# A four-layer linear-attention and memory-attention kernel: keys projected one tile ahead, weight remainders and memory updates moved, key features turned inside the next projection

## The chip, the cores and the metric

The kernel runs on one core of one Trainium2 chip. The metric is the device time of one execution in microseconds (us), the median of several runs; lower is better. TensorE (PE) multiplies matrices into eight PSUM banks; VectorE (DVE), ScalarE (ACT) and GpSimd (POOL) read, scale and write the results; SyncE (SP) issues most of the DMAs, the rest are issued by ACT and POOL. Each engine works through its own instructions in the order in which they are written, and waits on semaphores of the others.

## The reference

Four residual layers, A, B, A, B, act on x of 2048 tokens by 640 channels, with 32 heads of 20 channels:

```python
def _A_ref(x, wqkv, wo):                      # linear attention, no mask
    q, k, v = ...                             # x @ wqkv, by head
    phi = lambda t: jnp.where(t > 0, t + 1, jnp.exp(t)) + 1e-6
    pq, pk = phi(q), phi(k)
    kv = jnp.einsum("bhsd,bhse->bhde", pk, v)
    z = jnp.einsum("bhsd->bhd", pk)
    num = jnp.einsum("bhqd,bhde->bhqe", pq, kv)
    den = jnp.einsum("bhqd,bhd->bhq", pq, z)[..., None] + 1e-6
    return (num / den).reshape(B, S, D) @ wo
def _B_ref(x, wq, wk, wv, wo, beta):          # four segments of 512 tokens
    M, z = 0, 0                               # memory, 20 x 20 for a head
    for s in range(4):
        a_dot = softmax(qs @ ks.T * scale + causal_mask) @ vs
        a_mem = (phi(qs) @ M) / (phi(qs) @ z + 1e-6)
        outs.append(g * a_mem + (1 - g) * a_dot)
        M = M + phi(ks).T @ vs;  z = z + sum(phi(ks))
    return concat(outs) @ wo
x = x + _A_ref(_layernorm(x), A_wqkv, A_wo);  x = x + _B_ref(_layernorm(x), B_wq, ..., B_beta)
x = x + _A_ref(_layernorm(x), A_wqkv, A_wo);  x = x + _B_ref(_layernorm(x), B_wq, ..., B_beta)
```

## The kernel before

**Arithmetic.** The large products run on pairs of 16-bit parts. An operand is split into an upper half (ACT rounds it to 16 bits) and a lower half (DVE subtracts the upper from the original), and three of the four partial products are summed in PSUM: 15 matmuls for a tile of 128 tokens by 320 columns (line 416), or for 128 columns by 512 tokens (line 401). So a result goes PE, ACT, DVE, and only then can PE use it. Transposes, the weighing of values and the update of the memory are 32-bit matmuls.

**Stages.** The opening (0 to about 250 us) loads and splits the eight weight matrices and meanwhile does the first half of layer A: for each segment of four tiles, `g_first` projects keys (`keys(i)`) and queries (`queries(i)`), turns them into features, writes the queries' features to DRAM (`pqd`), and sums the product of features and inputs (`memory()`, line 592). After the last segment `merge` makes from that sum a 640 by 640 matrix `wm`. `a_second` reads the features back (`pqi`), normalizes and transposes them, multiplies by `wm` (line 416 with `wm,oT`) and adds the residual (`xo`, line 495). Layer B runs in the same stretch, segment by segment: `b_project` makes values, queries and keys, stores queries and keys to DRAM (`split_store`), and `attention` takes eight groups of four heads for a segment in slots of three stretches (table `STRETCHES`): row maxima (PE line 1026, DVE line 1032), scores (PE line 1067, ACT line 1071, POOL line 1078), weighing (`weigh`, line 1094), evacuation and normalizing (lines 1100 to 1118). Then comes layer A a second time (keys and queries about 760 to 1090 us, the first part of it beside the attention's last groups), and layer B again.

**The memory.** In `b_project` for each of five column tiles t, a query tile is projected, then the key features `pkT` of the tile before are transposed (`pk_turn`, line 884, copied by ACT at line 886), the key tile t is projected, and the memory of tile t-1 is updated (`update`, 16 small 32-bit matmuls, line 894, added to `acc` by DVE, lines 898 and 900). The fifth tile's turn and update are done by `rest()`, which the next segment's `a_second` draws in; there `masked` also copies `acc` into one of two buffers `mems` (line 751), which `read_mem` multiplies by the queries of the next segment.

**Order.** PE's order is exactly the order in which the program's two generators, `dense` (projections) and `attend` (attention slots), are drawn: each step returns a cost, and the generator with the lower total goes next. The other engines are ordered by a scheduler, from that order and estimated times; `high_priority` moves an instruction in it, and `issue_after` ties it behind another one on its engine.

**The handover.** At the end of the opening, the split of the last weight matrix, B's `wo`, has its five DVE lower halves (line 274, `w_Bo`) put late by `high_priority(offset=-1500)`; then it is written to DRAM as `wd_Bo` (line 279), and `open_b` waits for the last of them: one DVE memset of `one`, and six DMAs that write constant rows into the three key stacks `ks` (lines 847 to 850). These lines and `a_second`'s loads of `xo` (line 344) all stand in SP's queue.

Of the kernel before, what the change touches and what calls it, by code (L numbers as in the profile page):

```python
# [21 lines left out]
P = 128  # L22
# [122 lines left out]
class Kernel:  # L145
# [18 lines left out]
    def setup(self):  # L164
# [12 lines left out]
        self.mems, self.mn = [cp.tile([P, MW], F32, name=f"mem{j}") for j in range(2)], 0  # L177
# [56 lines left out]
    def w_prep(self, key, stage, w, wait=0, behind=None):  # L234
# [35 lines left out]
        for cols in (slice(0, HN), slice(HN, D)) if key == ("A", "k") else (slice(0, D),):  # L270
            for c in range(C):
                nc.scalar.activation(w[:, c, 0, cols], st[:, c, cols], AF.Copy, scale=scl)
                with self.tc.high_priority(offset=-1500) if key == ("B", "o") else nullcontext():
                    self.last = self.parted = nc.vector.scalar_tensor_tensor(w[:, c, 1, cols], st[:, c, cols], scl, w[:, c, 0, cols],
                                                               op0=OP.mult, op1=OP.subtract)
# [3 lines left out]
        nc.sync.dma_start(wd, w)  # L279
        self.wd[key] = wd  # L280
        yield 0.0
# [264 lines left out]
    def g_first(self, s, box, w, L, behind=None):  # L546
# [70 lines left out]
        if L["G"] is None and L["early"]:  # L617
# [123 lines left out]
    def masked(self, acc):  # L741


        mem = self.mems[self.mn % 2]
        self.mn += 1
# [97 lines left out]
    def open_stacks(self):  # L843
        nc = self.nc
        self.ks = [self.bp.tile([P, 2, SEG], F16, name=f"ks{j}") for j in range(3)]
        one = self.bp.tile([P, 2, SEG], F16, tag="nat", name="one", bufs=2)
        nc.vector.memset(one[:2], M_ONE)
        for k in self.ks:
            for a in (60, 124):
                nc.sync.dma_start(k[a:a + 2], one[:2])  # L850
# [15 lines left out]
    def b_project(self, st):  # L866
# [14 lines left out]
        def pk_turn():  # L881
# [3 lines left out]
            pk = bp.tile([P, SEG], F32, tag="pkt", name="pkt", bufs=1)  # L885
# [15 lines left out]

        for t in range(C):
# [17 lines left out]
            if pk is not None:  # L920
                update(t - 1, pk)
                yield 4 * 4 * E3 * COL
        st["projected"] = True

        def rest():
            if s == 0:
                yield from pause(4)
            if s < NSEG - 1:
                pk = pk_turn()
                yield 440  # L930
                update(C - 1, pk)
                yield 4 * 4 * E3 * COL
                st["mem"] = self.masked(acc)
        st["rest"] = rest()

# [187 lines left out]
    def attention(self, segs):  # L1123
# [3 lines left out]
        while n < NSEG * NG or prev or old:  # L1127
# [8 lines left out]
            for stretch in STRETCHES:  # L1136
                for op, k, back in stretch:
# [19 lines left out]
                    elif op == "sum":  # L1157
                        self.weigh(G, k)
# [266 lines left out]
```

## Time and profile before

| | |
|---|---|
| median of 3 runs (lowest, highest) | 1675.09 us (1674.74, 1676.49) |
| the profiled execution's own time, its span | 1673.65 us, 1671.6 us |
| PE busy | 1620.9 us (97%), 13818 matmuls |
| DVE, ACT, POOL busy | 1264.7 us (76%), 993.8 us (59%), 503.6 us (30%) |
| chain that ended last | PE 71%, DVE 14%, ACT 8%, DMA 3% |

The span runs from the first to the last instruction. A busy share is a mean over stages with different limits; PE's idle time is the rest of its row, 50.7 us. In rows of waits stand the engine and line that waited, the one it waited for, the total in us, how often, and the longest. In rows of the timeline stand the start in us, the length in us, the engine, the line, the operation, what it writes and reads, the shape, how many, and in brackets the engine's idle time before it and what ended it. In rows of windows stand the stretch, its length and for each engine the busy time, and then the clock that the throttle granted to PE (1.00 is full speed), the DMA engines' busy share and GB/s.

### The profile page before, as it was taken

The page shows a single profiled execution, that of the slowest core. Times are in us where ns is not written, and L with a number is a line of the kernel's source. Part 1 is how long each engine was busy: PE and PEld are TensorE (multiplying, and loading weights), DVE is VectorE, ACT ScalarE, POOL GpSimd, SP SyncE. Part 2 cuts the span into 40 slices and gives each one's busy share as a digit, 9 for nine tenths or more (in the row PEclk, how much of TensorE's full clock was granted, in tenths as well). Part 3 has the DMA queues.
Part 4 walks back from the last instruction along what each step waited for, and adds up shares of the span by engine and source line. Part 5 has one row for each costly group of instructions (what it writes and reads, how often), then busy time and mean ns, then how long its engine had stood idle before and what let it go on. Part 6 is the DMA issues. An engine that isn't in the chain of part 4 may idle for free.

```text
span 1671.6 us, 37870 instructions
## 1 busy us (share of the span) xinstructions
PE 1620.9 (97%) x13818; PEld 1016.7 (61%) x13818; DVE 1264.7 (76%) x4015; ACT 993.8 (59%) x1888; POOL 503.6 (30%) x1046
## 2 busy tenths in 40 slices
PE   8999998999999999999999999999999999999999
PEld 6767766464465566556557777765546646645555
DVE  7787896497887788769874465947889889878773
ACT  6666542357657647667666554333775676676673
POOL 4442241012323323433341210310232233232452
PEclk9999999999999999999999999999999999999999
DMA  6415654422322331461211303433232333323422
GB/s 223 158 53 188 220 199 173 141 98 75 118 73 71 125 115 61 137 205 56 81 45 45 114 33 125 180 98 128 78 113 90 108 95 109 108 85 105 147 100 96
DMA packets 110514, 190.98 MB, mean 114 GB/s; under 512 B 14188, under 2 KB 69868, under 8 KB 107768
## 3 DMA queue, kind: packets, MB, share of 16 engines
q1 hardware_dynamic: 97704, 142.68, 26.3%
q0 software_dynamic: 3264, 24.91, 4.2%
q10 hardware_dynamic: 9360, 20.98, 3.3%
q8 instruction: 109, 1.79, 0.4%
q14 instruction: 77, 0.63, 0.1%
HBM read 109.32 MB, written 78.64 MB: 112 GB/s over the span
## 4 chain that ended last, share of the span: by engine, by line
PE 71%; DVE 14%; ACT 8%; DMA 3%; issue 2%; POOL 1%; SPq 1%; ACTq 0%; DVEq 0%; POOLq 0%
PE ps L416 29%; PE ps L401 13%; PE ps L1094 8%; PE ps L592 4%; PE ps L1067 4%; PE ps L333 3%; ACT pe L1071 3%; PE ps L1026 3%; DVE ps L1032 3%; PE ps L469 2%; PE ps L1107 1%; DVE e L433 1%; DVE wmx L246 1%; DMA x<-in_A_x 1%; DVE pk L555 1%
## 5 line engine op out<-in xcount | busy, mean ns | idle before, releaser
L1032 DVE CUSTOM_DVE_ANT_0 ps<-ps,maskw 128x384 f32<-128x384 f32 (+3 forms) x1024 | 472.6, 520 | 31.7 <-PE ps L1026 27.4
L1071 ACT ACTIVATE pe<-ps,lsc 128x512 f32<-128x512 f32 x640 | 394.3, 694 | 82.1 <-PE ps L1067 66.7
L1078 POOL TENSOR_SCALAR_AFFINE_SELECT pe<-pe 128x256 f32<-128x256 f32 (+1 forms) x640 | 229.5, 364 | 412.5 <-ACT pe L1071 409.3
L416 PEld LDWEIGHTS <-xT 128*128 128x128 f16 x2880 | 279.8, 98 | 109.8 <-issue 4.5
L416 PEld LDWEIGHTS <-oT 128*128 128x128 f16 x1920 | 185.2, 98 | 87.3 <-issue 7.8
L1094 PE MATMUL ps<-pe,v 128*32 128x512 f32 (+3 forms) x2048 | 156.0, 436 | 7.7 <-ACT pe L1071 2.4
L416 PE MATMUL ps<-wm,oT 128*128 128x320 f16 x960 | 142.6, 301 | 4.5 <-DVE oT L338 4.2
L416 PE MATMUL ps<-w_Bo,oT 128*128 128x320 f16 x960 | 141.5, 299 | 3.8 <-ACT oT L337 2.0
L592 PE MATMUL ps<-pk,xs 128*128 128x321 f16 (+1 forms) x960 | 139.0, 302 | 5.2 <-DVE pk L555 2.5
L1032 DVE DVE_READ_ACCUMULATOR2_ANT mg<- 128x1 f32 x1024 | 143.9, 140 | 0.1
L401 PE MATMUL ps<-xT,w_Bq 128*128 128x512 f16 x600 | 140.9, 380 | 1.3 <-ACT pe L1071 0.8
L416 PE MATMUL ps<-w_Ak,xT 128*128 128x320 f16 x960 | 138.3, 299 | 1.5 <-DVE xT L338 0.9
L401 PE MATMUL ps<-xT,w_Bk 128*128 128x512 f16 x600 | 138.5, 379 | 1.2 <-ACT pe L1071 1.2
L416 PE MATMUL ps<-w_Bv,xT 128*128 128x320 f16 x960 | 139.3, 299 | 0.1
L416 PE MATMUL ps<-w_Aq,xT 128*128 128x320 f16 x960 | 137.8, 299 | 0.0
L1067 PE MATMUL ps<-qs,ks 62*128 62x512 f16 (+3 forms) x1024 | 129.5, 299 | 3.6 <-ACT pe L1071 2.2
L592 PEld LDWEIGHTS <-xs 128*128 128x128 f16 x960 | 93.4, 98 | 45.2 <-issue 3.0
L1026 PE MATMUL ps<-ks,qs 60*128 60x512 f16 (+3 forms) x1024 | 115.8, 297 | 3.0 <-DVE oT L338 1.8
L433 DVE SCALAR_TENSOR_TENSOR e<-e,r 128x320 f32<-128x320 f32 x128 | 68.1, 533 | 58.7 <-ACT r L432 58.2
L857 DVE SCALAR_TENSOR_TENSOR nat<-ps,nat 128x512 f16<-128x512 f32 x80 | 55.1, 689 | 65.3 <-ACT nat L856 65.0
L1094 PEld LDWEIGHTS ps<-pe,v 128*32 128x32 f32 x2048 | 62.9, 109 | 65.8 <-issue 47.0
L401 PEld LDWEIGHTS <-w_Bk 128*128 128x128 f16 x600 | 57.0, 98 | 67.3 <-issue 7.1
(202 smaller groups left out, 2367.0 us busy)
## 6 DMA issues: line engine op xcount, KB each, us to landing
x<-xn ACTq DMA_DIRECT2D x48, 320.0 KB
qs<-qd SPq DMA_DIRECT2D x128, 120.0 KB
ks<-kd SPq DMA_DIRECT2D x128, 120.0 KB
xo<-x SPq DMA_DIRECT2D x48, 320.0 KB
pqi<-pqd SPq DMA_DIRECT2D x32, 320.0 KB
qd<-nat SPq DMA_DIRECT2D x40, 256.0 KB
kd<-nat SPq DMA_DIRECT2D x40, 256.0 KB
x<-in_A_x SPq DMA_DIRECT2D x16, 320.0 KB
```

The source lines that it names most:

```text
L333: nc.tensor.transpose(pt[:, (c - c0) * P:(c - c0 + 1) * P], src[:, c * P:(c + 1) * P], self.ident)
L401: nc.tensor.matmul(p, w[:, c, a, t * P:(t + 1) * P], xT[:, c, b, :], start=k == 0, stop=k == 3 * C - 1)
L416: nc.tensor.matmul(p, xT[:, c, a, i * P:(i + 1) * P], w[:, c, b, n * HN:(n + 1) * HN], start=k == 0, stop=k == 3 * C - 1)
L433: nc.vector.scalar_tensor_tensor(e, e, 1.0, r, op0=OP.min, op1=OP.add)
L592: nc.tensor.matmul(p, xs[:, i, a, c * P:(c + 1) * P], pk[i][:, b, cols], start=i == 0 and a == b, stop=i == NT - 1 and a == 1)
L857: nc.vector.scalar_tensor_tensor(nat[:, 1], p, QK_SHIFT, nat[:, 0], op0=OP.mult, op1=OP.subtract)
L1026: nc.tensor.matmul(bs[par][:, a:a + n], qs[r, p, i * P:(i + 1) * P], ks[r, p, :n], start=True, stop=True)
L1032: nc.vector.tensor_tensor_reduce(bs[par][:, a:a + n], bs[par][:, a:a + n], self.maskw[:, SEG - n:], 1.0, NEG, OP.add, OP.max, G["mg"][:, p ...
L1067: nc.tensor.matmul(b[:, a:a + n], ks[r, p, j * P:(j + 1) * P], qs[r, p, j * P:], start=True, stop=True)
L1071: nc.scalar.activation(e, b, AF.Exp, scale=self.lsc)
L1078: self.select = nc.gpsimd.affine_select(d, d, pattern=pat, compare_op=OP.is_ge, fill=0.0, base=0, channel_multiplier=-1)
L1094: nc.tensor.matmul(G["pv"][32 * h4:32 * h4 + 32, j * P:], v[j][:, h * E1:h * E1 + 32], G.pop((p, par, j)), start=j == 0, stop=j == 2, skip ...
```

## The change

1. **Keys ahead** (`g_first`, all segments except the very first): the order k0 q0 k1 q1 k2 q2 k3 q3 becomes k0 k1 q0 k2 q1 k3 q2 q3. The last segment, whose queries 2 and 3 are drawn by `merge`, goes k0 k1 q0 k2 q1 k3.
2. **Handover**: the five lower halves of B's `wo` become `lower_parts()`, drawn last in the opening and tied behind the first turn of `a_second`'s tile 0. `wd_Bo` is no longer written. The three key stacks are filled whole by three POOL memsets, in place of a DVE memset and six DMAs.
3. **Updates**: a turned key tile's update is put on a list (`give`). The list is emptied in `attention` right after the last `weigh` of a group, and before a `pk_turn` where two updates are waiting (`take(1)`). `pkt` has two buffers in place of one.
4. **Turn**: `pk_turn` stands between the first 9 and the last 6 matmuls of the next key projection, not ahead of it. `rest()` has a pause between the turn and the copy `masked`.
5. `mems`, two buffers, becomes one, `mem`.

```diff
@@ w_prep @@
                 nc.scalar.activation(w[:, c, 0, cols], st[:, c, cols], AF.Copy, scale=scl)
-                with self.tc.high_priority(offset=-1500) if key == ("B", "o") else nullcontext():
-                    self.last = self.parted = nc.vector.scalar_tensor_tensor(w[:, c, 1, cols], ...
+                if key == ("B", "o"):
+                    continue
+                self.last = nc.vector.scalar_tensor_tensor(w[:, c, 1, cols], ...
...
+        if key == ("B", "o"):
+            self.remaining = (w, st, scl)
+            return
         wd = self.dr.tile([P, C, 2, D], F16, name="wd_%s%s" % key)
         nc.sync.dma_start(wd, w)
...
+    def lower_parts(self):
+        w, st, scl = self.remaining
+        behind = self.lower
+        for c in range(C):
+            with self.tc.high_priority(offset=-1500), self.tc.issue_after(behind.ins):
+                self.nc.vector.scalar_tensor_tensor(w[:, c, 1], st[:, c], scl, w[:, c, 0], op0=OP.mult, op1=OP.subtract)
+        yield 0.0
@@ g_first @@
+        yield from keys(0)
         for i in range(NT - 1):
-            yield from keys(i)
+            yield from keys(i + 1)
             if s < NSEG - 1 or i < 2:
                 yield from queries(i)
-        yield from keys(NT - 1)
@@ open_b @@
-        with self.tc.issue_after(self.parted.ins):
-            self.open_stacks()
...
-        one = self.bp.tile([P, 2, SEG], F16, tag="nat", name="one", bufs=2)
-        nc.vector.memset(one[:2], M_ONE)
         for k in self.ks:
-            for a in (60, 124):
-                nc.sync.dma_start(k[a:a + 2], one[:2])
+            self.nc.gpsimd.memset(k, M_ONE)
@@ b_project @@
-            pk = bp.tile([P, SEG], F32, tag="pkt", name="pkt", bufs=1)
+            pk = bp.tile([P, SEG], F32, tag="pkt", name="pkt", bufs=2)
...
+        def give(t, pk):
+            self.given.append(lambda: update(t, pk))
...
+            made = self.proj_t(xT, w["k"], t)
+            yield next(made)
             if pkT is not None:
+                yield self.take(1)
                 pk = pk_turn()
                 yield 440
-            p = yield from self.proj_t(xT, w["k"], t)
+            p = yield from made
...
             if pk is not None:
-                update(t - 1, pk)
-                yield 4 * 4 * E3 * COL
+                give(t - 1, pk)
...
             if s < NSEG - 1:
+                yield self.take(1)
                 pk = pk_turn()
                 yield 440
-                update(C - 1, pk)
-                yield 4 * 4 * E3 * COL
+                give(C - 1, pk)
+                yield 0.0
+                yield from pause(8)
+                yield self.take(0)
                 st["mem"] = self.masked(acc)
...
+    def take(self, keep):
+        n = len(self.given) if len(self.given) > keep else 0
+        for _ in range(n):
+            self.given.pop(0)()
+        return n * 16 * E3 * COL
@@ attention @@
                         self.weigh(G, k)
+                        if k == 2:
+                            self.take(0)
@@ opening @@
-                aux = chain(prep(("B", "k"), False), prep(("B", "o")), last(), self.a_head(L, 0, box))
+                aux = chain(prep(("B", "k"), False), prep(("B", "o")), last(), self.a_head(L, 0, box), self.lower_parts())
```

On PE the change adds and removes nothing: the same 13818 matmuls stand in another order. On the other engines it moves instructions at three places.

**Place one: VectorE at the end of the opening's second segment.** L555 and L568 are the same line of the two kernels, the lower half of a key tile's features (`pk`); L433 and L446 finish a feature, L582 and L595 add 1e-6 to a query's; L614 and L627 take the first product of `memory()`. Before:

```order
L433 SCALAR_TENSOR_TENSOR e<-e,r 128x320
L555 SCALAR_TENSOR_TENSOR pk<-e,k_scl,pk 128x320
L433 SCALAR_TENSOR_TENSOR e<-e,r 128x320
L555 SCALAR_TENSOR_TENSOR pk<-e,k_scl,pk 128x320
L433 SCALAR_TENSOR_TENSOR e<-e,r 128x320
L582 TENSOR_SCALAR e<-e 128x320
L433 SCALAR_TENSOR_TENSOR e<-e,r 128x320
L582 TENSOR_SCALAR e<-e 128x320
L614 TENSOR_TENSOR v_81<-ps,v_81 128x321
```

And now:

```order
L568 SCALAR_TENSOR_TENSOR pk<-e,k_scl,pk 128x320
L257 TENSOR_REDUCE wm_1402<-ps 1x1
L446 SCALAR_TENSOR_TENSOR e<-e,r 128x320
L595 TENSOR_SCALAR e<-e 128x320
L446 SCALAR_TENSOR_TENSOR e<-e,r 128x320
L595 TENSOR_SCALAR e<-e 128x320
L446 SCALAR_TENSOR_TENSOR e<-e,r 128x320
L595 TENSOR_SCALAR e<-e 128x320
L446 SCALAR_TENSOR_TENSOR e<-e,r 128x320
L595 TENSOR_SCALAR e<-e 128x320
L627 TENSOR_TENSOR v_80<-ps,v_80 128x321
```

Between the last key's lower half and `memory()` stand four halves of queries, where two stood.

**Place two: VectorE and SyncE at the handover.** `wm` is the merged matrix, `oT` the transposed features of `a_second`, `xn` its result. VectorE before:

```order
L274 SCALAR_TENSOR_TENSOR w_Bo<-stage,scl_Bo,w_Bo 128x640
L734 SCALAR_TENSOR_TENSOR wm<-ps,wm 128x320 x2
L338 TENSOR_TENSOR oT<-ps,oT 128x3x128
L338 TENSOR_TENSOR oT<-ps,oT 128x2x128
L847 MEMSET one 2x1024
L766 TENSOR_TENSOR pqi<-pqi,z 128x640
L770 TENSOR_REDUCE rca<-pqi 128x32
```

VectorE now:

```order
L747 SCALAR_TENSOR_TENSOR wm<-ps,wm 128x320 x10
L351 TENSOR_TENSOR oT<-ps,oT 128x3x128
L351 TENSOR_TENSOR oT<-ps,oT 128x2x128
L351 TENSOR_TENSOR oT<-ps,oT 128x3x128
L293 SCALAR_TENSOR_TENSOR w_Bo<-stage,scl_Bo,w_Bo 128x640
L778 TENSOR_TENSOR pqi<-pqi,z 128x640
L293 SCALAR_TENSOR_TENSOR w_Bo<-stage,scl_Bo,w_Bo 128x640
L782 TENSOR_REDUCE rca<-pqi 128x32
L508 SCALAR_TENSOR_TENSOR xn<-ps,ioG,xo 128x320
L783 TENSOR_SCALAR rca<-rca 128x32
L351 TENSOR_TENSOR oT<-ps,oT 128x2x128
```

The five lower halves of `w_Bo` have left the row of `wm` and stand among the first tiles of `a_second`. SyncE before:

```order
L756 DMA pqi<-pqd_0_96 128x640 x4
L279 DMA wd_Bo<-w_Bo 128x6400
L850 DMA ks_3346<-one 2x1024 x2
L850 DMA ks_3347<-one 2x1024 x2
L850 DMA ks_3348<-one 2x1024 x2
L344 DMA xo<-in_A_x 128x640 x4
```

Now `xo` follows the loads of `pqi` at once; nothing stands between them.

**Place three: ScalarE in an attention slot beside a projection.** `oTf` is the evacuation of a group, `nat` the first read of a finished projection, `e` and `r` its features. Before:

```order
L1100 ACTIVATE oTf<-ps,cg 128x512
L856 ACTIVATE nat<-ps 128x512
L1071 ACTIVATE pe<-ps,lsc 128x512
L440 ACTIVATE e<-ps,inv_Bk 128x512
L442 ACTIVATE r<-ps,inv_Bk 128x512
```

Now:

```order
L1119 ACTIVATE oTf<-ps,cg 128x512
L890 ACTIVATE pkt<-ps 128x512
L860 ACTIVATE nat<-ps 128x512
L1090 ACTIVATE pe<-ps,lsc 128x512 x2
L453 ACTIVATE e<-ps,inv_Bk 128x512
```

The copy of the turned key features, which stood behind the `nat` of the query projection before, stands ahead of the `nat` of the key projection. On PE the 30 updates stand in 21 blocks where they stood in 30: 9 blocks hold two, and 10 blocks stand directly behind the last matmuls of a weighing.

More of the change, by code (lines that the diff above doesn't have):

```diff
@@ L176, in setup @@
         self.blk = cp.tile([P, MW], BF16, name="blk")
-        self.mems, self.mn = [cp.tile([P, MW], F32, name=f"mem{j}") for j in range(2)], 0
+        self.mem = cp.tile([P, MW], F32, name="mem")
         self.wd, self.inv, self.scl, self.io = {}, {}, {}, {}
@@ L741, in masked @@
     def masked(self, acc):
[L744 to L745 removed]
+        mem = self.mem
         for (rel, t0, t1), c in zip(RUNS, (0, 0, 1, 1, 2, 2, 3, 3, 3)):
```

13 lines of the change are left out of this document (5 added, 8 removed).

## The prediction

> **What bounds the kernel now.** I read the page first, then PE's waits, then the stretches around the longest of them.
>
> ```profile
> span 1671.6 us, 37870 instructions
> PE 1620.9 (97%) x13818; PEld 1016.7 (61%) x13818; DVE 1264.7 (76%) x4015; ACT 993.8 (59%) x1888; POOL 503.6 (30%) x1046
> ...
> PE 71%; DVE 14%; ACT 8%; DMA 3%; issue 2%; POOL 1%; SPq 1%; ACTq 0%; DVEq 0%; POOLq 0%
> ```
>
> PE is busy for 97% of the span and carries 71% of the chain that ended last. Since the change gives PE the same matmuls, it can only win from PE's 50.7 us of idle time, and from matmuls that run slower than they could. The table of PE's waits says where the idle time lies:
>
> ```profile
> PE ps L416 <- DVE oT L338: 5.0, 6, 2.4
> PE ps L592 <- DVE pk L555: 2.5, 3, 2.0
> PE ps L1094 <- ACT pe L1071: 2.4, 6, 0.7
> PE ps L894 <- ACT pe L1071: 2.4, 6, 0.4
> PE ps L894 <- ACT pkt L886: 2.3, 6, 0.4
> PE ps L401 <- ACT pe L1071: 2.0, 5, 0.4
> PE ps L884 <- DVE pkT L443: 1.3, 2, 1.0
> PE ps L592 <- ACT pk L568: 0.8, 1, 0.8
> PE ps L333 <- DVE acc L898: 0.7, 2, 0.3
> PE ps L1094 <- DVE acc L900: 0.5, 2, 0.3
> ```
>
> No single wait is large; those that name this change's lines (338 at the handover, 555 and 568, 894, 884, acc) come to some 15 us. Behind two of them lies a second loss, which shows only in the granted clock:
>
> ```profile
> 111.00:114.50 3.50, 3.02 (x16) 1.93 (x17) 2.65 (x6) 2.23 (x5) 0.92 (x2) 0.74 0.00 0
> 114.50:118.00 3.50, 3.50 (x21) 2.15 (x20) 2.11 (x8) 0.10 (x1) 1.12 (x2) 0.77 0.25 94
> 252.00:253.50 1.50, 0.27 (x2) 0.15 (x3) 1.50 (x4) 0.00 (x0) 0.00 (x0) 0.71 0.82 290
> 253.50:257.00 3.50, 3.50 (x19) 2.19 (x18) 3.17 (x7) 0.21 (x1) 0.07 (x1) 0.64 1.04 267
> 870.00:1090.00 220.00, 219.51 (x1724) 158.03 (x1719) 135.96 (x309) 110.82 (x232) 45.55 (x91) 1.00 0.28 97
> ```
>
> Each row ends with PE's granted clock, DMA's share and GB/s. The clock falls after the two longest pauses. Clock lost: 3.5 x 0.26 + 3.5 x 0.23 = 1.7 us at 111, and 1.5 x 0.29 + 3.5 x 0.36 = 1.7 us at 252. The last row is layer A's second time: 0.5 us of 220 idle, so reordering can win nothing there.
>
> [...] A closed pause is therefore worth more than its length.
>
> **The change part by part.**
>
> *Keys ahead.* The long pause at 111 us is the end of the second segment, where `memory()` waits for the last key tile:
>
> ```profile
> 102.92 4.24 PE L416 MATMUL ps<-w_Aq,xT 128*128 128x320 f16 x30
> 107.00 1.40 PE L592 MATMUL ps<-pk,xs 128*128 128x321 f16 x9
> 109.21 0.31 PE L592 MATMUL ps<-pk,xs 128*128 128x321 f16 x1 [0.82 <-ACT pk L568]
> 111.48 4.86 PE L592 MATMUL ps<-pk,xs 128*128 128x321 f16 x22 [1.96 <-DVE pk L555]
> 109.19 2.23 DVE L555 SCALAR_TENSOR_TENSOR pk<-e,k_scl,pk 128x320 f16<-128x320 f32 x1 [0.63 <-ACT pk L568]
> 108.84 1.41 POOL L500 TENSOR_TENSOR xs<-xh,xs 128x640 f16<-128x640 f32 x1
> ```
>
> The last key's projection ended at 102.9, its first lower half was ready at 111.4; DVE was late, and that half itself took 2.23 us beside a POOL subtraction. Thirty query matmuls, 4.1 us, covered it. Now sixty stand there, 8.2 us: 4.1 us more cover against 0.82 + 1.96 = 2.78 us of waiting. DVE's queue between holds two query halves more, but behind the last key's half, so they don't delay it. Value: -2.8 for the pauses and -1.7 for the clock, -4.5. Bounds: -4.5, and 0 if DVE is later by as much as the cover grew. I take -4.4. In the other segments of both A layers the same wait is 0.2 us or not there; there I take 0, with +-1.5 for the part at 760 to 870 us that shares ACT and DVE with attention.
>
> *Handover.* In the order of time, PE, DVE and SP:
>
> ```profile
> 253.23 3.30 PE L416 MATMUL ps<-wm,oT 128*128 128x320 f16 x13 [2.38 <-DVE oT L338]
> 265.85 2.04 PE L416 MATMUL ps<-wm,oT 128*128 128x320 f16 x13 [1.84 <-DVE oT L338]
> 251.04 0.87 DVE L274 SCALAR_TENSOR_TENSOR w_Bo<-stage,scl_Bo,w_Bo 128x640 f16<-128x640 f32 x1
> 252.63 0.87 DVE L338 TENSOR_TENSOR oT<-ps,oT 128x384 f16<-128x384 f32 x2
> 264.31 1.01 DVE L495 SCALAR_TENSOR_TENSOR xn<-ps,ioG,xo 128x320 f32<-128x320 f32 x2 [6.69 <-DMA xo<-in_A_x]
> 251.98 0.32 SPq L279 DMA_DIRECT2D wd_Bo<-w_Bo  x1
> 254.60 4.88 SPq L850 DMA_DIRECT2D ks<-one  x6
> 259.53 5.38 SPq L344 DMA_DIRECT2D xo<-in_A_x  x4
> ```
>
> First pause: four `w_Bo` halves, 0.8 us or more each, stand between the `wm` halves ahead of `oT`. Without them `oT` is at most 3.2 us earlier, but no earlier than the last `wm` product lets it: I leave 0.3 us of the 2.38, so -2.1 and, with no long pause, -1.7 of clock. Second pause: DVE sat 6.69 us for `xo`, whose loads SP issued only at 259.53, behind `wd_Bo` and six small DMAs that waited for the memset; PE ran on until the next `oT` stood behind that. SP now goes from `pqi` straight to `xo`, with neither the store nor the six DMAs between. So -1.84. The five halves cost 5 x 0.87 = 4.4 us of DVE among the first tiles, less than its 6.69 us of idle time there. What waits now: `xn` stands ahead of the second part of tile 1's `oT` on DVE, so if `xo` were late, PE would still stall; `xo` was 4.8 us from its first issue to its use, and is needed once the first tile's two halves are multiplied, 30 matmuls of 0.14 us or 4 us in, so I keep +0.5. Sum -5.1; bounds -5.6 and 0.
>
> The three memsets of `ks` go on POOL, ahead of the second tile's 1/sigma, and start once the last `w_Bo` half has freed the memory under them. Their price is not in the trace; the nearest rows:
>
> ```profile
> L684 POOL MEMSET kt<- 128x128 f16 x10 | 2.1, 215 | 7.4 <-PE ps L592 7.2
> L1258 POOL MEMSET mem<- 128x756 f32 x2 | 1.4, 728 | 0.0
> ```
>
> By elements (0.73 to 0.95 ns each) 1024 take 0.85 to 1.0 us, by bytes (2048 of them) 0.6: 1.8 to 3.0 us for three. Nearest is the large one, by elements: 3 us. PE turns that tile only after the next one's 30 matmuls, over 4 us: 0, at worst +1.
>
> [...]
>
> *Updates and turns.* Rows of layer B: an update straight after a projection, one in an attention slot, and the same point of a slot that has no update:
>
> ```profile
> 311.02 3.40 PE L401 MATMUL ps<-xT,w_Bk 128*128 128x512 f16 x15
> 314.35 0.65 PE L894 MATMUL ps<-v,pkt 128*32 128x63 f32 x32
> 1229.69 0.65 PE L894 MATMUL ps<-v,pkt 128*32 128x63 f32 x32 [0.40 <-ACT pe L1071]
> 1216.20 2.10 PE L401 MATMUL ps<-xT,w_Bq 128*128 128x512 f16 x9 [0.40 <-ACT pe L1071]
> ```
>
> - `rest()`: turn, copy and update follow each other, six waits for the copy. The pause and the list put other matmuls between: -2.3.
> - Turns that wait for `pkT`, twice, 1.3: nine matmuls of 0.22 us, 2 us, now stand ahead of them: -1.3.
> - Updates that wait for `pe`, 2.4: the last two rows show that this pause takes whatever comes at this point, an update or, without one, the next query projection. It is a wait for a bank of PSUM. I expect it to pass to the projection: 0, at best -2.4. The same question stands for the banks that `acc` frees (0.7 + 0.5): half, -0.6.
> - Entering the small tiles: 15 matmuls at 0.216 us are 3.24, the update began after 3.33; 0.09 us each. 30 entries become 21, of which 10 follow a weighing, which uses the same 32-column tiles: between 9 and 19 x 0.09, I take -1.3.
> - Against it: turns and updates now take banks while a key projection still holds one, and the update delays the next row maxima by its 0.58 us. By the rows above a missing bank costs 0.40. 24 turns and 10 updates are so placed: 0 to 34 x 0.40 = 13.6. Where updates move to, right after a weighing, the slot's earlier banks have been read, so I take the low part, +2.
>
> Sum of this part -3.2. The single `mem` makes `masked` wait for the reads of the old memory, but the code has it behind them already: 0.
>
> **Sum.** -4.4 - 5.1 - 3.2 = -12.7 us, against the profiled execution's own 1673.65 (span 1671.6 and 2.05 around it): 1660.95. That execution was 1.44 us below the median of the runs, 1675.09, so for a median I predict 1675.09 - 12.7 = 1662.4.
>
> **The rivals.**
>
> - *Layer B nets nothing.* [...] As a mechanism of this kernel: all the 0.4 us pauses are for banks, and each passes to the next matmul that needs one. For it: the twin rows above. Against it: `pkt` and `pkT` are waits for data. Only the opening is won, -9.5: 1665.6. 17%.
> - *The handover only moves its stall.* `xo` comes late all the same, since DMA is 82% to 104% busy from 252 to 257 us, and five `w_Bo` halves hold up `oT`; the clock falls again. -12.7 + 5.1 = -7.6: 1667.5. 13%.
> - *Keys ahead don't help.* DVE stays behind by the added query work: -12.7 + 4.4 = -8.3: 1666.8. 8%.
> - *Slower: the held bank.* Each of the 34 turns and updates put inside an open key projection or ahead of the row maxima stalls PE for a bank. At 0.7 us, the longest wait of a weighing for ACT, that is 23.8 in place of my +2: -12.7 - 2 + 23.8 = +9.1: 1684.2. It decides from 0.53 us each, where 18 us cancel the 14.7 and exceed 0.2%. Against it: the pause at 0.40 is the same wherever it occurs. 10%.
>
> **How the numbers follow.** My forecast has 52%, with a range of its own of 1657 to 1668. A difference of 0.2%, 3.35 us, is about what a measurement of this kernel tells from no change: faster is below 1671.7, slower above 1678.4. Faster: nearly all of the forecast (50), most of the first three rivals (28 of 38): 0.78. Same: the remainder of these and a third of the held bank, 0.13. Slower: 0.09. The low end, 1656, is the forecast with the bank pauses and the whole of the entries won (-3) and layer A's -1.5, and a little of the bank price; the high end, 1674.5, is the handover's rival with 7 us of bank pauses. Outside lie about 2 in 10.
>
> **What would show it.** Right: no fall of the clock at 111 and 252 us, no wait of line 592 for `pk` over 0.3 us in the second segment, `xo` issued before 255 us, rows "894 <- pkt" and "884 <- pkT" gone, and "401 <- pe" grown to about 4 us in 11. Wrong: a clock below 1.00 after 20 us, a pause at the second or third tile of `a_second` for `oT` or `xn`, new waits of lines 884 and 401 for `pe` of more than 2 us in all, or row maxima (1026, 1032) late behind updates.

## The result, and the profile after

The changed kernel takes 1662.97 us (median of 5 runs, 1662.16 to 1665.72), the kernel before 1675.09 us beside it: 0.9927 of its time, 95% interval 0.9914 to 0.9940. The prediction was 1662.4 us. A second measurement (below) gave 1664.01 us; over all ten runs the median is 1663.6. The execution profiled here was the longest of its five, 1665.72 us; the last section says why.

In the changed kernel's profile the lines around the change stand 4 to 19 higher: 416 is 429, 401 is 414, 592 is 605, 333 is 346, 884 is 888, 894 is 898, 1067 is 1086, 1071 is 1090, 1094 is 1113. The head of its page and its chain:

```profile
span 1664.0 us, 37840 instructions
PE 1618.3 (97%) x13818; PEld 1020.6 (61%) x13818; DVE 1256.1 (75%) x4014; ACT 994.3 (60%) x1888; POOL 508.5 (31%) x1048
...
PE 76%; DVE 11%; ACT 7%; issue 2%; DMA 2%; POOL 1%; SPq 0%; ACTq 0%; DVEq 0%; POOLq 0%
```

PE's idle time fell from 50.7 to 45.7 us, and its busy time, with the same matmuls, by 2.6; of the chain that ended last it carries 76% where it carried 71%, VectorE 11% where it was 14%. What it waits for now:

```profile
PE ps L1113 <- ACT r L455: 6.2, 7, 1.3
...
PE ps L414 <- ACT pe L1090: 2.8, 7, 0.4
PE ps L1113 <- ACT pe L1090: 2.6, 7, 0.5
PE ps L346 <- ACT pe L1090: 2.2, 5, 0.5
...
PE ps L346 <- POOL pqi L786: 1.5, 1, 1.5
...
PE ps L429 <- DVE oT L351: 0.9, 4, 0.4
PE ps L888 <- ACT pe L1090: 0.7, 2, 0.4
...
PE ps L605 <- DVE pk L568: 0.5, 1, 0.5
```

The waits that the change aimed at are gone or small: for `oT` 5.0 before, 4.2 of it at the handover, and 0.9 now, none of it there, for `pk` 2.5 and 0.5 (at 39 us, in the first segment, whose order stayed), for `pkt` (2.3) and `pkT` (1.3) none. At the head stands a wait that had been 1.3 us: a weighing (1113) for ScalarE's `r`. The same two stretches as before, and two where the clock falls now:

```profile
111.00:114.50 3.50, 3.50 (x27) 2.40 (x25) 3.31 (x10) 2.56 (x7) 1.59 (x3) 1.00 0.24 88
...
246.00:250.00 4.00, 3.82 (x29) 2.52 (x27) 3.96 (x8) 1.35 (x4) 0.15 (x1) 1.00 1.02 426
...
1367.00:1370.50 3.50, 3.31 (x9) 1.17 (x9) 3.38 (x12) 3.03 (x6) 2.64 (x5) 0.51 0.48 139
1605.50:1609.00 3.50, 2.94 (x12) 1.98 (x13) 2.51 (x9) 2.79 (x6) 1.62 (x4) 0.56 0.04 11
```

At 111 and from 246 to 250 PE is all but fully busy at a clock of 1.00. In this execution the clock falls at 1367 and 1605 instead, which costs 3.5 x 0.49 = 1.7 us and, as far as it lies in the second row, 3.5 x 0.44 = 1.5 us (the whole stretch, 1605.92 to 1609.33, costs 1.7 too). The handover itself, PE, SyncE's queue and GpSimd:

```profile
246.37 2.53 PE L429 MATMUL ps<-wm,oT 128*128 128x320 f16 x15
...
231.30 24.84 SPq L357 DMA_DIRECT2D xo<-in_A_x  x4
...
258.45 2.73 POOL L854 MEMSET ks<- 128x1024 f16 x3 [1.61 <-DVE w_Bo L293]
```

The first product runs without a pause, `xo` is issued from 231 us on (259.5 before), and the three memsets take 2.73 us together.

Where the time was won, the starts of the same matmuls in both traces show. From the start to the first value projection of layer B the changed kernel is 9.75 us shorter, in the first layer B, up to the first key projection of its last segment, 2.65 (its third segment alone gives 2.69); from there to the second layer B, most of it the second layer A, it is 1.2 us longer, and the second layer B is 3.6 longer, of which 3.4 are the two stretches of half clock. Together that is the 7.6 us between the two spans. The execution profiled in the second measurement has the same 2.65 and 1.2, is 10.4 us shorter in the opening and 2.2 longer in the second layer B, with 1.8 us of half clock there.

### The profile page after: what moved, and what is told of

It is laid out like the page before. It is cut to its first block, busy times and chain, and to the rows that moved or that the text cites. A ratio compares the mean times of both kernels' runs of the same rounds, so it can differ in the third digit from the quotient of the medians.

```text
span 1664.0 us, 37840 instructions
## 1 busy us (share of the span) xinstructions
PE 1618.3 (97%) x13818; PEld 1020.6 (61%) x13818; DVE 1256.1 (75%) x4014; ACT 994.3 (60%) x1888; POOL 508.5 (31%) x1048
## 4 chain that ended last, share of the span: by engine, by line
PE 76%; DVE 11%; ACT 7%; issue 2%; DMA 2%; POOL 1%; SPq 0%; ACTq 0%; DVEq 0%; POOLq 0%
PE ps L429 30%; PE ps L414 14%; PE ps L1113 9%; PE ps L605 4%; PE ps L1086 4%; PE ps L346 4%; PE ps L1045 3%; ACT pe L1090 3%; PE ps L482 2%; DVE ps L1051 2%; PE ps L1126 2%; DVE e L446 1%; DMA x<-in_A_x 1%; PE ps L888 1%; ACT xh L401 1%
## 5 line engine op out<-in xcount | busy, mean ns | idle before, releaser
L1086 PE MATMUL ps<-qs,ks 62*128 62x384 f16 (+3 forms) x1024 | 130.5, 299 | 3.6 <-ACT pe L1090 2.2
L446 DVE SCALAR_TENSOR_TENSOR e<-e,r 128x320 f32<-128x320 f32 x128 | 64.8, 507 | 58.9 <-ACT r L445 58.2
L414 PEld LDWEIGHTS <-w_Bq 128*128 128x128 f16 x600 | 57.1, 98 | 69.1 <-issue 10.9
```

The source lines that it names most:

```text
L414: nc.tensor.matmul(p, w[:, c, a, t * P:(t + 1) * P], xT[:, c, b, :], start=k == 0, stop=k == 3 * C - 1)
L446: nc.vector.scalar_tensor_tensor(e, e, 1.0, r, op0=OP.min, op1=OP.add)
L1086: nc.tensor.matmul(b[:, a:a + n], ks[r, p, j * P:(j + 1) * P], qs[r, p, j * P:], start=True, stop=True)
```

## The experiments

All times are medians. The ratios and their intervals are those on record; they are not the quotients of the two medians beside them (for the handover alone that quotient is 0.9983). "Alone" means the kernel before with one piece of the change; the other experiments start from the changed kernel.

**Keys ahead, alone.** The kernel before with the new order in `g_first`:

```diff
+        yield from keys(0)
         for i in range(NT - 1):
-            yield from keys(i)
+            yield from keys(i + 1)
             if s < NSEG - 1 or i < 2:
                 yield from queries(i)
-        yield from keys(NT - 1)
```

> The kernel before with the keys one tile ahead, and nothing else of the change. Theory (the terms of the prediction add up): the wait of 2.8 us for the last key tile and the half clock behind it (1.7 us) are gone at the end of the opening's second segment, so the first matmul with wm and oT comes 4 to 5 us earlier than before; the handover's two pauses stay, and later parts stay within 1.5 us: 1670 to 1672 us in all. Rival (keys ahead only moves VectorE's lateness): that point is earlier by less than 1.5 us, 1673.5 us or more.

Measured: 1670.95 us against 1674.71, ratio 0.9976 (0.9964 to 0.9987). Stretches of its trace at the old place, and at the handover, which is as before:

```profile
111.00:114.50 3.50, 3.50 (x27) 2.40 (x26) 3.31 (x9) 2.29 (x6) 1.70 (x3) 1.00 0.25 94
247.50:251.00 3.50, 2.81 (x12) 1.58 (x13) 3.24 (x6) 0.00 (x0) 0.00 (x0) 0.62 0.98 267
```

The pause and the half clock at 111 us are gone, those of the handover stay. The first product of `a_second` starts 5.05 us earlier than in the kernel before, and the head start is 5.4 at the first value projection of layer B. Between 690 and 1090 us, in the second layer A, 0.9 of it is given back, most of that where its projections run beside the attention's last groups (up to some 800 us).

**Handover, alone.** `lower_parts()`, no `wd_Bo`, three memsets:

```diff
+                if key == ("B", "o"):
+                    continue
...
+            self.nc.gpsimd.memset(k, M_ONE)
...
+                aux = chain(prep(("B", "k"), False), prep(("B", "o")), last(), self.a_head(L, 0, box), self.lower_parts())
```

> The kernel before with the handover's part alone (the five lower halves of w_Bo behind the first turn, no wd_Bo, ks by three GpSimd memsets). Theory: the two pauses at 253 and 266 us (2.4 and 1.8 us) and the half clock between (1.7 us) go, 5 to 6 us from there on: 1669 to 1670.5 us, with the wait at 111 us unchanged. Rival (the loads of xo stay late because the DMA engines are busy, so the second pause only moves): 2 to 4 us, 1671 to 1673 us, with a wait of TensorE for oT at the second or third tile.

Measured: 1671.87 us against 1674.71, ratio 0.9972 (0.9960 to 0.9984).

```profile
111.00:114.50 3.50, 3.05 (x13) 1.80 (x14) 2.66 (x6) 2.23 (x5) 0.91 (x3) 0.61 0.00 0
...
251.00:254.50 3.50, 3.32 (x25) 2.15 (x24) 3.46 (x7) 1.32 (x4) 0.18 (x1) 1.00 1.04 420
```

Now it is the other way round: the clock falls at 111 us and holds at the handover. From the first product of `wm` to the first of `w_Bv` PE is 5.7 us shorter than before, the same as in the changed kernel. By its time alone, 1671.87 us, this run lies where the rival was expected (1671 to 1673); the trace decides against that rival, since PE's waits of line 429 for `oT` come to 0.6 us in all. In this execution the stretch began 1.0 us later than in the kernel before, and of the 4.7 us of head start behind it 3.2 are left at the end.

**Updates and turns, alone.** Points 3, 4 and 5 of the change; `g_first`, `w_prep` and `open_b` as before.

> The kernel before with the memory's part alone (updates on the list, the turn inside the next key projection, one mem, two pkt). Theory: layer B wins what the changed kernel won there, 2 to 3.5 us in all, as the sum of about 8 us of waits and tile entries won and about 5 us of new waits of the weighing for ScalarE: 1671.5 to 1673 us. Rival (layer B wins nothing by itself; what it showed in the changed kernel came from the earlier parts, by other meetings of the two streams): 1674.5 to 1676 us.

Measured: 1674.07 us against 1674.71, ratio 0.9992 (0.9978 to 1.0006): no difference that this measurement can tell, and neither the expected 1671.5 to 1673 nor the rival's 1674.5 to 1676. In its trace the first layer B is 2.9 us shorter than before, the second 0.2 longer; the opening, which this part does not touch, was 1.5 us longer in this execution. Its table of PE's waits has the changed kernel's new head:

```profile
PE ps L1108 <- ACT r L442: 6.2, 7, 1.3
...
PE ps L592 <- DVE pk L555: 2.4, 2, 2.0
```

So the 6.2 us come from this part; the opening's wait for `pk` is as it was. Where from, two slots of the same weighing show. Before, PE and then ACT:

```profile
406.17 1.06 PE L1094 MATMUL ps<-pe,v 128*32 128x512 f32 x8 [0.16 <-ACT r L442]
...
403.34 0.67 ACT L856 ACTIVATE nat<-ps 128x512 f16<-128x512 f32 x1
403.81 0.68 ACT L886 ACTIVATE pkt<-ps 128x512 f32<-128x512 f32 x1
404.76 0.69 ACT L440 ACTIVATE e<-ps,inv_Bq 128x512 f32<-128x512 f32 x1 [0.27 <-DVE nat L857]
405.35 0.68 ACT L442 ACTIVATE r<-ps,inv_Bq 128x512 f32<-128x512 f32 x1
```

And after:

```profile
396.68 1.07 PE L1113 MATMUL ps<-pe,v 128*32 128x512 f32 x8 [1.33 <-ACT r L455]
...
393.88 0.63 ACT L860 ACTIVATE nat<-ps 128x512 f16<-128x512 f32 x1
395.27 0.69 ACT L453 ACTIVATE e<-ps,inv_Bq 128x512 f32<-128x512 f32 x1 [0.76 <-DVE nat L861]
395.85 0.68 ACT L455 ACTIVATE r<-ps,inv_Bq 128x512 f32<-128x512 f32 x1
```

The weighing doesn't use `r`. In the program its bank of PSUM is, in all seven cases, the one in which the query projection was made, and `r` is the last operation that reads it. So this is a wait for a held bank. Before the change a turn (0.44 us of PE) stood between that projection and the weighing; now the turn comes after it, and PE arrives at the weighing before ACT is through. That is not the whole of the 1.17 us by which this wait grew: counted from where PE leaves the query projection (402.71 and 392.48 us), PE arrives 0.43 us earlier, and `r` ends 0.73 us later, since ScalarE starts the projection's `nat` 1.40 us behind that end where it was 0.63.

**The turn ahead of the whole key projection**, in the changed kernel:

```diff
             made = self.proj_t(xT, w["k"], t)
-            yield next(made)
             if pkT is not None:
                 yield self.take(1)
                 pk = pk_turn()
                 yield 440
             p = yield from made
```

> The changed kernel with one thing undone: the turn of the key features stands ahead of the next key projection again, all 15 matmuls behind it; the updates stay on the list. Theory: the weighing's new waits for ScalarE (6.2 us in 7 against 1.3 in 5 before) come from the turn's 0.44 us missing between the query projection and the weighing, so that TensorE arrives before the exponentials; they fall to 1.5 to 3 us, the waits for pkT (1.3 us) come back: 1 to 3.5 us faster than the changed kernel. Rival (the waits come from where the updates stand): they stay at 5 us or more, and the time is the same as or up to 2 us above the changed kernel.

Measured: 1663.61 us, ratio 0.9928 (0.9906 to 0.9949), by the median the time of the changed kernel; the gain of 1 to 3.5 us that was expected did not come.

```profile
PE ps L888 <- DVE pkT L456: 2.3, 7, 0.8
...
PE ps L1111 <- ACT pkt L890: 1.4, 2, 0.7
...
PE ps L1111 <- ACT r L455: 0.9, 3, 0.6
```

The wait for `r` falls from 6.2 to 0.9 as the mechanism says, and the waits for `pkT` and `pkt` are back. By segments, from the starts of the same matmuls in both traces, the middle one of each layer B was 0.95 us shorter than in the changed kernel and the first 1.4 longer. The third was 2.0 us longer in the first layer B and 2.9 shorter in the second, where the changed kernel's execution had a stretch of half clock (1.7) and a wait of 1.5 us that this one lacks. The turn's place is a trade, and it falls out differently in each segment. Three of this run's four executions had a mean granted clock of 1.000 and took 1663.28 to 1663.67 us; the changed kernel's four at 1.000 took 1662.16 to 1662.97. So the turn inside the projection may still be worth about 1 us in all.

**Without the updates' part**: the changed kernel with points 3, 4 and 5 undone.

> The changed kernel without its memory part: keys ahead and handover stay, updates, turns, pkt and mem are as before. Keys ahead alone gave 0.9976 and the handover alone 0.9972 of the kernel before, 4.1 and 3.2 us, so they should give about 1667.3 us if they add up. Theory (the memory part wins its waits for data and gives most of that back to weighings that wait for ScalarE): this kernel is 1 to 3 us above the changed kernel, 1664 to 1666 us. Rival 1 (the parts simply add up, and the rest comes from the memory part): 4 us or more above it, 1667 or more. Rival 2 (the memory part nets nothing at all): the same as the changed kernel, 1662.4 to 1663.4. In every case PE's waits of line 894 for pkt (2.3 us) and of 884 for pkT (1.3 us) are there again under this kernel's line numbers, and the 6.2 us of the weighing for ScalarE's r is back at 1 to 1.5 us.

Measured: 1665.34 us, ratio 0.9939 (0.9926 to 0.9952).

```profile
PE ps L899 <- ACT pkt L891: 2.3, 6, 0.4
...
PE ps L1099 <- POOL pe L1083: 1.8, 2, 0.9
...
PE ps L889 <- DVE pkT L456: 1.3, 2, 1.0
PE ps L1099 <- ACT r L455: 1.3, 5, 0.6
```

The old waits are back, `r` is at 1.3. The changed kernel is 2.4 us below this (1.3 by its second measurement, on another chip), and the intervals of the ratios, 0.9926 to 0.9952 here and 0.9914 to 0.9940 there, overlap. The executions at a mean clock of 1.000 are further apart: four here took 1664.83 to 1665.54 us, four of the changed kernel 1662.16 to 1662.97, some 2.7 less. In the traces, from the first value projection of layer B to the end is 1399.0 us here, without half clock, and 1398.6 and 1397.2 in the changed kernel's two, 3.4 and 1.8 of them lost to half clock. So in this company the third part is worth perhaps 1 to 3 us; the times alone do not prove it. The first two add up within the measurement: 0.9976 x 0.9972 = 0.9948 against 0.9939. (The 4.1 and 3.2 us in the expectation are not what was measured: the medians give 3.8 and 2.8, the ratios 4.0 and 4.7.)

**Only the queue's part of the handover**: the kernel before without `wd_Bo` and with GpSimd's memsets; the five lower halves of `w_Bo` stay among the `wm` halves.

> The kernel before with only the queue part of the handover: wd_Bo is not written, and the three key stacks are filled by GpSimd in place of a VectorE memset and six transfers; the five lower halves of w_Bo stay among the wm halves. Theory (two causes, one for each pause): the second pause at 265.9 us (1.84 us) goes, because xo is issued straight behind pqi; the first (2.38 us at 253.2) stays with the half-rate window behind it; 1.5 to 2.5 us less than the kernel before, ratio 0.9985 to 0.9991. Rival 1 (the two pauses have one cause, the lower halves, and the second is only the first's after-effect): no gain, ratio 1.000. Rival 2 (the queue was the cause of both): the whole of the handover's gain, 3.2 us or more, ratio 0.998 or less.

Measured: 1673.21 us against 1676.70, ratio 0.9985 (0.9975 to 0.9994). PE's wait for `oT` falls from 5.0 to 3.1 us; the longest left, 2.4, is the first pause:

```profile
PE ps L418 <- DVE oT L340: 3.1, 5, 2.4
```

So the two pauses have two causes. This execution had no half clock behind the first pause (1.00 from 250 to 261 us); others of its twelve runs may have had it, since they lie between 1670.67 and 1676.33 at mean clocks of 1.000 to 0.997.

**The lower halves early again**, in the changed kernel:

```diff
-                if key == ("B", "o"):
-                    continue
-                self.last = nc.vector.scalar_tensor_tensor(...
+                with self.tc.high_priority(offset=-1500) if key == ("B", "o") else nullcontext():
+                    self.last = nc.vector.scalar_tensor_tensor(...
...
-                aux = chain(..., self.a_head(L, 0, box), self.lower_parts())
+                aux = chain(..., self.a_head(L, 0, box))
```

> The changed kernel with the five lower halves of w_Bo among the wm halves again, as before the change; all else as changed (the loads of xo at once behind pqi, no store, GpSimd's memsets). Theory (the halves alone make the first pause of the handover): PE waits about 2.1 to 2.4 us for oT near 245 us, and in part of the executions a half-rate window follows; 2 to 4 us more than the changed kernel on the same chip, 1664.5 to 1667 us, and a wider scatter. Rival 1 (VectorE was late there for another reason, which keys ahead removed): no pause, same as the changed kernel within 1 us. Rival 2 (the five late halves cost DVE time in a_second's first tiles that they save ahead of oT): the same again or a little less than the changed kernel, though the pause is there.

The changed kernel itself ran beside it and the last experiment:

> The changed kernel itself, unchanged, once more, so that the next two runs stand beside it on one chip. Theory: 1662.2 us in an execution without a half-rate window and 1.7 us more for each window; with no pause of over 1.6 us left in the trace after the start, most executions have none or one: median 1662 to 1664 us and a scatter under 4 us, where the kernel before, with four pauses of 1.8 to 2.4 us, scatters by 6 us or more.

Measured on one chip: the changed kernel 1664.01 us (1662.58 to 1666.57), with the halves early 1665.87 (1662.83 to 1666.17).

```profile
PE ps L428 <- DVE oT L350: 2.8, 5, 2.1
...
247.50:251.00 3.50, 3.27 (x14) 2.04 (x15) 2.52 (x5) 0.00 (x0) 1.75 (x2) 0.58 0.90 366
251.00:254.50 3.50, 3.50 (x27) 2.65 (x26) 2.51 (x7) 0.87 (x2) 1.27 (x1) 0.93 0.43 138
```

The first pause is back with 2.1 us, and behind it 3.5 x 0.42 + 3.5 x 0.07 = 1.7 us of half clock; in this trace the first value projection of layer B starts 3.1 us later than in the changed kernel beside it. The two medians alone, 1.9 us apart with ranges that overlap, would not show it. Of what was expected of the changed kernel itself, the median came just outside (1662 to 1664) and the scatter of 4.0 us just inside; but the kernel before, for which 6 us or more were expected, scattered by only 3.1 us beside it, in nine executions.

**The turn first in the middle segment alone**, after what the segments had shown:

```diff
             made = self.proj_t(xT, w["k"], t)
-            yield next(made)
+            if s != 1:
+                yield next(made)
```

> The changed kernel with the turn ahead of the whole key projection in the middle segment alone, and inside the projection in the others. With the turn ahead in all segments the time was that of the changed kernel; by segments the middle one was about 1 us better in each layer B, the other two worse. Theory (in the middle segment the turn's 0.44 us between a query projection and the weighing is what gives ScalarE time for r): the wait of line 1113 for r (6.2 us in 7) falls to under 2 us, and the time falls by 1 to 2 us, to about 1661 us. Rival (the waits only change their names, as in the run with all turns ahead): same as the changed kernel, 1662.4 to 1663.4, with waits of 888 for pkT and of 414 for pe in place of the 6.2 us.

Measured: 1662.38 us (1661.41 to 1663.79), ratio 0.9921 (0.9907 to 0.9935). The wait for `r` fell to 0.9 us in 3, but the time, expected at about 1661, can't be told from the changed kernel's on another chip.

**No empty step ahead of a turn.** The draw `take(1)` gives a step of no length when nothing is on the list, and what runs beside the projection is drawn once more there. In the changed kernel that brings the next segment's first turn to PE too soon. PE and GpSimd:

```profile
1365.49 0.55 PE L346 MATMUL ps<-ident,pqi 128*128 128x128 f32 x3 [1.55 <-POOL pqi L786]
...
1363.90 0.29 POOL L1097 TENSOR_SCALAR_AFFINE_SELECT pe<-pe 128x128 f32<-128x128 f32 x1 [0.29 <-ACT pe L1090]
1364.16 3.73 POOL L786 TENSOR_TENSOR pqi<-pqi,rca 128x640 f32<-128x640 f32 x3
```

The three products of `pqi` are tied behind the last select, which ended at 1364.2, and the turn waits 1.55 us for the first.

```diff
             if pkT is not None:
-                yield self.take(1)
+                cost = self.take(1)
+                if cost:
+                    yield cost
```

> The changed kernel where the draw ahead of a turn is no step of its own when there is nothing on the list, so that what runs beside the projection is drawn one step less there. Theory (the empty step lets the next layer's head draw its pqi too early, behind GpSimd's last select): PE's wait for pqi of line 786 (1.5 us in the last segment) goes, with the half-rate window behind it in the executions that had one; 1.5 to 2.5 us less than the changed kernel, about 1661 us. Rival (the head arrives early all the same, or the wait is taken by something else of the last segment): same as the changed kernel within 0.5 us.

Measured: 1662.85 us, ratio 0.9922 (0.9908 to 0.9935). The wait for `pqi` is gone, yet there is no gain that can be told (about 1661 us was expected): in the third segment of the first layer B, where the changed kernel gains 2.7 us on the kernel before, this one gained only 1.0.

**Both pieces where each wins**: the turn first in the middle segments, no empty step in the third segment of the last layer alone.

```diff
+            if s != 1:
+                yield next(made)
...
+                cost = self.take(1)
+                if cost or s < 2 or not st["last"]:
+                    yield cost
```

> The changed kernel with the turn ahead of the whole key projection in the middle segment alone (as in the run before that did this), and without the empty step in the third segment of the last layer B. Theory: the first piece wins about 1.6 to 0.9 us in the middle segment of each layer B, the second the 1.5 us wait for pqi at 1365 us and its window; together 2 to 4 us less than the changed kernel on the same chip, 1659 to 1661 us, and the wait for pqi is gone from PE's table. Rival: the gains are given back where dense work and attention share ScalarE later on, as part of the first layer's gain was in the change itself: within 1 us of the changed kernel.

Measured: 1660.58 us (1659.93 to 1661.82), ratio 0.9910 (0.9895 to 0.9925). All its runs lie below the lowest of the changed kernel's ten, 1662.16, and its median is 3.4 us below that of the changed kernel on the same chip. The two profiled executions there have one stretch of half clock each, and their spans differ by 2.7 us, so the gain is not one of the clock. What PE waits for:

```profile
PE ps L414 <- ACT pe L1093: 2.4, 6, 0.4
...
PE ps L1116 <- ACT r L455: 0.9, 3, 0.6
```

No row for `pqi` is left. This version beats both kernels.

## Why the prediction was right, and where its steps were off

**Keys ahead, -4.4.** Measured -3.8 by the medians alone and -5.1 at the first product of `a_second`. Pauses and half clock went together, as worked out; 0.9 us is lost again in the second layer A, inside the +-1.5 that the step kept. The rival "keys ahead don't help" has fallen.

**Handover, -5.1.** Measured -5.7 between the first product of `wm` and the end of that segment, of 120 products; -4.7 by the ratio and -2.8 by the medians alone, so the step's size rests on the trace. The two causes that the step named were told apart: the queue's part takes away the second pause, the lower halves make the first (2.1 us when put back, the very 2.1 of the step) with 1.7 of clock. The +0.5 kept for a late `xo` was not needed, as `xo` came 28 us earlier. The memsets, priced at 3 us, took 2.73. The rates given for them were misread: 728 ns for 756 elements are 0.96 ns each and 215 for 128 are 1.7, not 0.73 to 0.95; the measured 0.91 us for 1024 is 0.89 ns each. GpSimd's next result reached VectorE 0.9 us late, and PE did not wait for it. The rival "only moves its stall" has fallen.

**Updates and turns, -3.2.** The step's own terms add up to -3.5; with them the sum would have been -13.0 and the forecast 1662.1. Measured -0.6 alone, with an interval that holds no change, -1.3 to -2.4 beside the other parts, and some -2.7 between executions at full clock: the times do not settle the size. Its terms come apart in the traces. Before, the two groups:

```profile
L894 PE MATMUL ps<-v,pkt 128*32 128x63 f32 x960 | 19.5, 221 | 4.7 <-ACT pe L1071 2.4 <-ACT pkt L886 2.3
L884 PE MATMUL ps<-ident,pkT 128*128 128x128 f32 x120 | 18.3, 275 | 1.6 <-DVE pkT L443 1.3 <-PE ps L401 0.2
```

After:

```profile
L898 PE MATMUL ps<-v,pkt 128*32 128x63 f32 x960 | 17.6, 219 | 0.2
L888 PE MATMUL ps<-ident,pkT 128*128 128x128 f32 x120 | 18.7, 278 | 0.9 <-ACT pe L1090 0.7 <-DVE tmp L1136 0.2
```

- Waits for `pkt` and `pkT`: -3.6 priced, -3.6 measured. Both rows are gone.
- Entering the small tiles: -1.3 priced; the updates' busy time fell from 19.5 to 17.6, -1.9 (that of the turns rose by 0.4). Whether the fewer entries are the cause was not tested.
- Bank pauses of 2.4 that pass to others: 0 priced. Passed they have: the turns wait 0.7, the projections 2.8 for 2.0, the transposes 2.2 for 0.8, the weighings 2.6 for 2.4, in all +0.7. They did not gather at line 414 with some 4 us, as the list of signs had it, but spread over three lines.
- Banks of `acc`: -0.6 priced, -1.2 measured; both rows are gone.
- Held banks: +2 priced, +4.9 measured (weighings for `r`, 1.3 to 6.2). This is the mis-sized term. The mechanism was the fourth rival's, and at its places it costs more than the 0.7 that rival gave it (6.2 / 7 = 0.9). But it strikes at 7 places, not at 34, and all are weighings in the slot of a query projection. The step looked for a bank that the moved turn holds; in fact PE lost the turn as cover and reached the bank early, and in the slot shown ScalarE was also later by 0.7 us.
- Two things the step did not have: the 1.5 us wait for `pqi`, from the empty step, and a gain, weighings that waited 1.8 us for GpSimd's select and no longer do.

These make -3.6 - 1.9 + 0.7 - 1.2 + 4.9 + 1.5 - 1.8 = -1.4, within what the runs give; they are the rows that the step named and the largest others, not all. By the lengths of the stages the part won 2.65 us in the first layer B and, with the half clock taken off, nothing in the second (0.2 longer than before). The total, -12.1 against -12.7, came out nearer than its terms. The first two parts together gave 10 to 11 us where 9.5 were priced, the third probably less than its price, and each median also depends on how many stretches of half clock, of 1.7 us each, its executions had: so near a hit is in part luck. The rival "layer B nets nothing", by which the 0.4 us pauses only change owner, was half right: the pauses for banks that wait on `pe` passed on, those for data did not. Its time, 1665.6, is what the kernel without this part took (1665.34), and by the medians it is not clearly beaten.

Of the signs, those of "right" were seen but for the last: the projections' wait for `pe` grew from 2.0 to 2.8 us, not to 4. One of those of "wrong" was seen too, a clock below 1.00 after 20 us: at 1367, behind the wait for `pqi` that the change itself made, and at 1605.

## What to carry to other kernels

Price a pause of TensorE together with the half clock that may follow it (here 3.41 us at 0.50, 1.7 us lost), and ask of each what is late there, queue by queue: here three pauses had three causes (too little cover, an operation ahead on VectorE, a transfer behind others on SyncE), and closing them, with the half clock behind them, made most of the gain: 0.9939 of the time without the third part. An instruction moved out of a slot is also cover taken from the next wait there: before moving it, ask which bank the following matmul takes, who reads that bank last, and when that reader gets its turn. And look at segments apart, since the place that is best in one can lose as much in another.

## What was not expected of the hardware

The half clock doesn't come in every execution. The kernel before, with pauses of 2.0, 2.4 and 1.8 us, took 1672.93 to 1681.89 us in all its runs beside the experiments; the changed kernel 1662.16 to 1666.57. Its four runs at a mean clock of 1.000 took 1662.16 to 1662.97, its three at 0.998 1664.99 to 1666.57. Set to their edges, the rows show that a stretch is 3.41 us long at 0.50, which costs 1.7. In the kernel before, one begins in the handover's first pause, and none follows the second:

```profile
252.63:256.04 3.41, 2.81 (x11) 1.60 (x12) 3.15 (x6) 0.00 (x0) 0.00 (x0) 0.50 1.07 289
262.87:266.28 3.41, 1.57 (x13) 1.04 (x12) 1.97 (x5) 0.38 (x1) 0.00 (x0) 1.00 0.53 175
266.28:269.69 3.41, 3.41 (x27) 2.40 (x25) 3.09 (x10) 1.12 (x2) 0.57 (x1) 1.00 0.67 242
```

In each of the two kernels' executions the starts of the stretches lie whole multiples of 3.413 us apart: 112.68 and 252.63 in the kernel before 41 of them (139.95 us), 1366.99 and 1605.92 in the changed kernel 70 (238.93 us). Between the two executions, both counted from the start of the span, the starts are 1.6 us out of step. The wait for `oT`, 2.4 us long in both, came with a half clock in the kernel before and without one in the run with the queue's part alone; why, no run shows.

Nor does it need a long pause. In the last experiment, PE and the stretch behind it:

```profile
1599.25 0.32 PE L1089 MATMUL ps<-qs,ks 62*128 62x384 f16 x1 [0.50 <-ACT pe L1093]
...
1600.40 0.38 PE L1089 MATMUL ps<-qs,ks 62*128 62x384 f16 x2 [0.20 <-ACT pe L1093]
1601.47 0.57 PE L346 MATMUL ps<-ident,otok 128*128 128x128 f32 x3 [0.69 <-DVE oT L351]
...
1601.80:1605.21 3.41, 3.41 (x15) 1.98 (x14) 1.62 (x7) 1.90 (x4) 1.54 (x4) 0.50 0.00 0
```

Three pauses of 0.50, 0.20 and 0.69 us within 3 us, and the clock is 0.50 for the next 3.41. So 2.1 us in one piece (with the lower halves early again), or 1.4 in three, were followed by a half clock in some executions.

How much idling tips it, the traces do not settle. In the 3.41 us ahead of the two kernels' four half clocks PE had been idle for 1.96 and 1.82 us in the kernel before, and for 1.73 and 1.26 in the changed kernel. As long a stretch with 1.84 us idle (262.87 in the kernel before, above) and one with 1.34 (1209.98 in the changed kernel) were followed by full clock. So the idle time of PE alone does not decide it; what else does was not tried.
